# Landing margins per kind of transfer, eight early weight conversions instead of eleven, and the gathers of the row sums issued by GpSimd

## The chip, the core and the metric

The kernel runs on one core of a Trainium2 chip. The metric is the device time of one execution in microseconds (us), the median of several runs. The core has TensorE (PE, matmuls), VectorE (DVE), ScalarE (ACT), GpSimd (POOL) and SyncE (SP, which here only issues DMAs); each works through its own instructions in order and waits at an instruction whose inputs are not there.

## What is computed

Attention on 4 batches of 12 heads (448 tokens, 64 features a head), with scores capped by a tanh, and two feed-forward layers on its output, seen as 1792 tokens of 768 features.

```python
def _attn_ref(q, k, v, cap):
    scores = scale * np.matmul(q, k.transpose(0, 1, 3, 2))
    scores = cap * np.tanh(scores / cap)
    scores = scores - np.max(scores, axis=-1, keepdims=True)
    attn = np.exp(scores)
    attn = attn / (np.sum(attn, axis=-1, keepdims=True) + 1e-09)
    return np.matmul(attn, v).astype(np.float32)

def _moe_ref(x, w_in, w_out):           # d_ff 2048
    h = np.maximum(x @ w_in, 0.0)
    return (h * h @ w_out).astype(np.float32)

def _moe2_ref(x, w_gate, w_val, w_out): # d_ff 1536
    gate = 1.0 / (1.0 + np.exp(-(x @ w_gate)))
    val = x @ w_val
    return (gate * val @ w_out).astype(np.float32)
```

q, k, v are float32; the five weight matrices arrive as float64.

## The kernel before

**Attention** runs over 24 pairs of heads (`pairs`; `last` is 23). For each pair PE makes the scores in four steps (L339, tiles `so`, `si`, `se`), the products with v (L400, `pvo`) and the row sums (L416, `pvs`). ACT makes tanh and exp (`pt`). DVE splits q and k into a rounded part and a rest (L247 and L235, `qkh`, `qkl`) and takes both PSUM results out (L244, `xe`). Then the row sums go round: they sit on single partitions of `xe`, four small DMAs gather them onto 16 partitions (L442, `sg<-xe`, 1.8 KB each), DVE adds and inverts them (L444, L446), the result goes to DRAM (`rd<-rr`), comes back spread over the partitions (L452, `th<-rd`, two DMAs), DVE multiplies (L456), and the product is stored (`xn<-xe`). Two `sg` tiles and two `th` tiles are in use.

**Weights.** Each of the 68 float64 tiles (768 KB) is loaded as pairs of words (L614, `w<-in_w_dram`), turned into float32 by `convert` (L617 on) and stored to DRAM (`s_w<-raw`). Its steps are an absolute value (L627 on DVE during attention; on ACT once the event `mlp` has come, L625), two short DVE steps (L629, L631) and two long ones (L633, L635). Two `w64` and two `raw` tiles exist. `load_w` reads the float32 tiles back when a `pair` tile is free (L661); ACT and DVE split them into `wh` and `wl` (L771, L776) for three matmuls a product (L785, L787, L788, `pb`). `convert_all` (L603) says when a float64 tile is loaded: the first eleven after the pairs 2, 4, ... 22, the rest by the unit of matmuls at which the tile is needed, less 70 units.

**The feed-forward layers** run on four column blocks (stages) with seven products in place of eight; their matmuls are the PE's units.

**The order** of every engine is written before the program runs: a planner (`Flow`) plays the kernel through with durations of its own and writes each engine's instructions in the order in which they come there. A load's landing is `landing` (L162): the transfer at a rate, a latency, and `DLAG`, a margin of 0.3 us. What the planner gets wrong is not mended on the chip: the order stays, and engines wait in it.

Of the kernel before, what the change touches and what calls it, by code (L numbers as in the profile page):

```python
# [19 lines left out]
SP = 512  # L20
NP = H // 2
P = 128
# [7 lines left out]
SR = 32  # L30
EARLY = 150
TWO = (0, 1, 2)
DLAG = 0.3
EDGE = {(0, 2): (0, 0), (1, 0): (0, 2), (1, 2): (1, 0), (2, 0): (1, 2)}
BEGIN = 1
WARM = 3

PT, XE, TH, NV, WB = 2, 6, 2, 2, 4
WSTART, PACE, AHEAD, FIRST = 2, 2, 70, 130
R, G, CP, TM, GX, GY = 5, 5, 3, 3, 8, 4  # L40
HK = CC // 2
HALF = (0, HK, 1)
# [18 lines left out]
class Flow:  # L61
# [2 lines left out]


    LAG = 0.05
    LAND = {"in": (270e3, 1.05), "load": (350e3, 1.15), "store": (350e3, 0.85), "th": (234e3, 1.3), "rd": (350e3, 1.4),
        "sg": (350e3, 0.8)}
    OVER = {"ACT": 0.1, "DVE": 0.08, "SP": 0.0}

    def __init__(self, have):
        self.now, self.heap, self.turn = 0.0, [], 0
        self.have, self.taking = dict(have), {}
        self.done, self.until = {}, []
        self.queue = {e: [] for e in ("ACT", "DVE", "SP")}
        self.free = {e: True for e in self.queue}
        self.pipe = 0.0
        self.changed = lambda: None
        self.jobs = 0
# [34 lines left out]
    def serve(self, engine):  # L114
# [10 lines left out]
        self.at(self.now + length + self.LAG, lambda: self.step(job))  # L125
        self.at(self.now + max(0.02, length - self.OVER[engine]), end)

# [34 lines left out]
    def landing(self, size, kind="load"):  # L162
        rate, after = self.LAND[kind]
        self.pipe = max(self.now + 0.5, self.pipe) + size / rate
        return self.pipe + after + DLAG - self.now


@with_exitstack
def attn_mlp_kernel(ctx: ExitStack, tc: tile.TileContext, qk, v, cap, w1, w2, wg, wv, wo, out):
    nc = tc.nc  # L170
# [8 lines left out]
    def open_pool(name, side, **kw):  # L179
        guard = tc.tile_pool(name=name, bufs=1, side=side, **kw)  # L180
        open_pools[name] = guard, guard.__enter__()

    def close_pool(name):
        open_pools.pop(name)[0].__exit__(None, None, None)

    def T(pool, tag, shape, dt=F32, bufs=1):
        pool = wp if pool == "wp" else open_pools[pool][1]
        return pool.tile(shape, dt, tag=tag, name=tag, bufs=bufs, align_bytes=ALIGN)
# [25 lines left out]
    for j in range(2):  # L214
# [3 lines left out]
    flow = Flow({  # L218
        "sb": 3, "pvo": 1, "pvs": 1, "v": NV, "qkh": 2, "qk": 2, "pt0": PT, "pt1": PT, "xe": XE, "th": TH, "sg": 2,
        "w64": 2, "raw": 2, "pair": 2, "sums": 2, "wh": WB, "tm": TM, **{x: HK for x in FORM.values()},  # L220
        "acc": CC, "gx": GX, "gy": GY, "r": R, "g": G, "cp": CP, "pb": 0})
# [6 lines left out]
    def on(engine, length, write, rank=1):  # L228
        return "on", engine, length, write, rank
# [13 lines left out]
    def copy_ps(out, in_, rank=0):  # L243
        return on("DVE", flow.dve(cols(out)), lambda: nc.vector.tensor_copy(out, in_), rank)  # L244
# [5 lines left out]
    def dma(out, in_, size, kind="load", issue=0.42, rank=1):  # L250
        yield on("SP", issue, lambda: nc.sync.dma_start(out=out, in_=in_), rank)
        yield "for", flow.landing(size, kind)
# [5 lines left out]
    rd = [[dr.tile([2, S], F32, name=f"rd_{b}_{p}") for p in range(NP)] for b in range(B)]  # L258
    xn = [dr.tile([P, B * S], F32, name=f"xn_{p}") for p in range(NP)]
    yn = [dr.tile([P, 2 * BW], F32, name=f"yn_{c}") for c in range(CC)]  # L260
    RP, RN = 16, 2 * S // 16
    pairs = [(b, p) for b in range(B) for p in range(NP)]
    last = len(pairs) - 1
# [156 lines left out]
    def result(n, o):  # L420
        flow.put("pt0")
        flow.put("pt1")
        b, p = pairs[n]
        yield "until", ("xe", n)
        xe = st["xe", n]
        yield copy_ps(xe[:, 1], o)
        flow.put("pvs")
        flow.fire(("pv", n))
        if n == last:
            close_pool("att")  # L430
            open_pool("mlp", "right")
            flow.fire("mlp")


        yield "take", "sg"
        sg = T("out", "sg", [RP, 2, RN], bufs=2)
        rr = T("out", "rr", [RP, RN], bufs=2)
        for x in range(2):
            for j in range(2):
                r0 = (2 * x + j) * SR  # L440
                src = xe[r0:r0 + 1, 1].rearrange("o (i s) -> o i s", s=RN)
                yield on("SP", 0.65, lambda: nc.sync.dma_start(out=sg[j * RP // 2:(j + 1) * RP // 2, x], in_=src), 0)  # L442
        yield "for", flow.landing(0, "sg")
        yield on("DVE", 0.26, lambda: nc.vector.scalar_tensor_tensor(  # L444
            out=sg[:, 0], in0=sg[:, 0], scalar=eps[:RP], in1=sg[:, 1], op0=ALU.add, op1=ALU.add), 0)
        yield on("DVE", 0.49, lambda: nc.vector.reciprocal(rr, sg[:, 0]), 0)  # L446
        yield from dma(rd[b][p].rearrange("r (i s) -> (r i) s", s=RN), rr, 0, "rd", rank=0)
        flow.put("sg")
        yield "take", "th"
        bc = T("out", "th", [P, S], bufs=TH)  # L450
        for j in range(2):
            yield on("SP", 0.52, lambda: nc.sync.dma_start(  # L452
                out=bc[j * D:(j + 1) * D], in_=rd[b][p][j].unsqueeze(0).to_broadcast((D, S))), 0)
        yield "for", flow.landing(P * S * 4, "th")
        xu = xe[:, 0]
        yield on("DVE", flow.dve(S), lambda: nc.vector.tensor_tensor(out=xu, in0=xu, in1=bc, op=ALU.mult), 0)  # L456
        flow.put("th")
        yield from dma(xn[p][:, b * S:(b + 1) * S], xu, P * S * 4, "store", rank=0)
        flow.put("xe")
        flow.fire(("stored", "x", b, p))  # L460
        st["normal"] = st.get("normal", 0) + 1
        if st["normal"] == len(pairs):
            close_pool("out")
            open_pool("sum", "left")
            open_pool("mlp2", "right")
            flow.fire("sum")
# [136 lines left out]
    def convert_all():  # L603
        second_half = [key for key in keys if key[0] not in ("w1", "w2")]
        begin, end = first[second_half[0]] - FIRST, first[second_half[-1]] - AHEAD
        for m, key in enumerate(keys):
            n, u = WSTART + PACE * m, first[key] - AHEAD
            if key in second_half:
                u = min(u, begin + (end - begin) * second_half.index(key) // len(second_half))
            yield "until", ("t", n, 3) if n < last else ("unit", max(u, 0))  # L610
            src, n = source(key)
            yield "take", "w64"
            w64 = T("wp", "w64", [P, CC * P, 2], U32, bufs=2)[:, :n]
            yield on("SP", 0.42, lambda: nc.sync.dma_start(out=w64.rearrange("p n x -> p (n x)"), in_=src.bitcast(U32)), 2)  # L614
            flow.spawn(convert(key, w64, flow.landing(P * n * 8, "in")))

    def convert(key, w64, wait):  # L617
        yield "for", wait
        yield "take", "raw"
        lo, hi = w64[:, :, 0], w64[:, :, 1]  # L620
        n = w64.shape[1]
        raw = T("wp", "raw", [P, CC * P], bufs=2)[:, :n]
        mu = raw.bitcast(U32)
        if "mlp" in flow.done:
            yield act(raw, hi.bitcast(F32), AF.Abs)  # L625
        else:
            yield on("DVE", flow.dve1(n), lambda: nc.vector.tensor_scalar(  # L627
                out=mu, in0=hi, scalar1=0x7FFFFFFF, scalar2=None, op0=ALU.bitwise_and), 2)
        yield on("DVE", flow.dve1(n), lambda: nc.vector.tensor_scalar(  # L629
            out=raw, in0=raw, scalar1=LOW, scalar2=HIGH, op0=ALU.max, op1=ALU.min), 2)  # L630
        yield on("DVE", flow.dve1(n), lambda: nc.vector.tensor_scalar(  # L631
            out=mu, in0=mu, scalar1=5, scalar2=2, op0=ALU.logical_shift_left, op1=ALU.logical_shift_right), 2)
        yield on("DVE", flow.dve(n), lambda: nc.vector.scalar_tensor_tensor(  # L633
            out=mu, in0=lo, scalar=29, in1=mu, op0=ALU.logical_shift_right, op1=ALU.bitwise_or), 2)
        yield on("DVE", flow.dve(n), lambda: nc.vector.scalar_tensor_tensor(  # L635
            out=mu, in0=hi, scalar=0xC0000000, in1=mu, op0=ALU.bitwise_and, op1=ALU.bitwise_or), 2)
        flow.put("w64")
        kind, i = key
        name = f"s_{kind}_{i}".translate({ord(x): "_" if x == "," else None for x in " ,()"})
        scratch[key] = dr.tile([P, n], F32, name=name)  # L640
        yield from dma(scratch[key], raw, P * n * 4, "store")
        flow.put("raw")
        flow.fire(("kept", key))
# [370 lines left out]
    units, groups, first, spot = [], [], {}, {}  # L1014
# [279 lines left out]
```

## Time and profile before

| | |
|---|---|
| median of 3 runs | 1116.3 us (1112.49 to 1118.37) |
| the profiled execution | 1117.42 us, its span 1115.6 us |
| PE busy | 1097.2 us (98% of the span) |
| PE weight loads | 919.6 us (82%) |
| DVE | 899.1 us (81%) |
| ACT | 688.3 us (62%) |
| POOL | 1.1 us, 10 instructions, all memsets of the first 2 us |
| DMA | 227.42 MB, mean 204 GB/s |

A matmul's busy time overlaps the next one's, so a busy share near 100% doesn't tell how much PE lost; its waits and the steps of its sequence do. Attention takes the first 200 us or so, the layers the rest.

### The profile page before, as it was taken

The page shows a single profiled execution, that of the slowest core. Times are in us where ns is not written, and L with a number is a line of the kernel's source. Part 1 is how long each engine was busy: PE and PEld are TensorE (multiplying, and loading weights), DVE is VectorE, ACT ScalarE, POOL GpSimd, SP SyncE. Part 2 cuts the span into 40 slices and gives each one's busy share as a digit, 9 for nine tenths or more (in the row PEclk, how much of TensorE's full clock was granted, in tenths as well). Part 3 has the DMA queues.
Part 4 walks back from the last instruction along what each step waited for, and adds up shares of the span by engine and source line. Part 5 has one row for each costly group of instructions (what it writes and reads, how often), then busy time and mean ns, then how long its engine had stood idle before and what let it go on. Part 6 is the DMA issues. An engine that isn't in the chain of part 4 may idle for free.

```text
span 1115.6 us, 16096 instructions
## 1 busy us (share of the span) xinstructions
PE 1097.2 (98%) x5706; PEld 919.6 (82%) x5706; DVE 899.1 (81%) x1532; ACT 688.3 (62%) x1154; POOL 1.1 (0%) x10
## 2 busy tenths in 40 slices
PE   9999899999999999999999999999999999999998
PEld 4444444798989998999989998998999999999997
DVE  4677999888977488788897999989988767568687
ACT  7889899567464556675656656656545355555352
POOL 0000000000000000000000000000000000000000
PEclk9999999999999999999999999999999999999999
DMA  4678886888875266778896617385438932331322
GB/s 144 210 230 276 253 268 208 266 300 272 260 238 199 65 234 209 286 278 275 319 344 223 223 57 255 135 297 170 163 148 294 323 100 71 104 123 64 100 71 99
DMA packets 83984, 227.42 MB, mean 204 GB/s; under 512 B 11840, under 2 KB 29888, under 8 KB 83904
## 3 DMA queue, kind: packets, MB, share of 16 engines
q1 hardware_dynamic: 83904, 226.40, 60.1%
q8 instruction: 45, 0.74, 0.3%
q14 instruction: 35, 0.29, 0.1%
HBM read 160.24 MB, written 65.95 MB: 203 GB/s over the span
## 4 chain that ended last, share of the span: by engine, by line
PE 75%; DVE 11%; DMA 9%; ACT 3%; issue 2%; SPq 1%; DVEq 0%; POOL 0%; ACTq 0%; POOLq 0%
PE pb L785 21%; PE pb L787 21%; PE pb L788 21%; PE pvo L400 5%; DMA s_w<-raw 2%; PE pvs L416 2%; DVE wl L235 2%; PE se L339 2%; PE so L339 2%; PE si L339 2%; DVE raw L635 1%; ACT wh L232 1%; DVE acc L976 1%; DMA sg<-xe 1%; DVE raw L633 1%
## 5 line engine op out<-in xcount | busy, mean ns | idle before, releaser
L787 PE MATMUL pb<-gx,wh 128*128 128x448 f32 x564 | 205.9, 365 | 1.3 <-DVE gx L235 1.3
L788 PE MATMUL pb<-gx,wh 128*128 128x448 f32 x564 | 205.8, 365 | 0.0
L785 PE MATMUL pb<-gx,wl 128*128 128x448 f32 x564 | 205.1, 364 | 0.0
L785 PE MATMUL pb<-t,wl 128*128 128x448 f32 x480 | 176.2, 367 | 4.3 <-ACT cp L232 4.0
L787 PE MATMUL pb<-t,wh 128*128 128x448 f32 x480 | 175.6, 366 | 0.0
L788 PE MATMUL pb<-t,wh 128*128 128x448 f32 x480 | 175.2, 365 | 0.0
L232 ACT ACTIVATE wh<-pair 128x384 fp32r<-128x384 f32 (+1 forms) x182 | 111.5, 628 | 81.6 <-PE pb L788 63.6
L232 ACT ACTIVATE wh<-sums 128x384 fp32r<-128x384 f32 (+1 forms) x172 | 90.7, 542 | 109.8 <-PE pb L788 88.5
L235 DVE TENSOR_TENSOR wl<-pair,wh 128x384 fp32r<-128x384 f32 (+1 forms) x182 | 123.5, 689 | 26.4 <-ACT wh L232 25.8
L785 PE MATMUL pb<-b,wl 128*128 128x448 f32 x360 | 132.6, 368 | 3.0 <-ACT pb L232 2.8
L787 PE MATMUL pb<-b,wh 128*128 128x448 f32 x360 | 132.5, 368 | 0.0
L788 PE MATMUL pb<-b,wh 128*128 128x448 f32 x360 | 132.0, 367 | 0.0
L235 DVE TENSOR_TENSOR wl<-sums,wh 128x384 fp32r<-128x384 f32 (+1 forms) x172 | 97.7, 579 | 31.9 <-ACT wh L232 31.5
L787 PEld LDWEIGHTS pb<-gx,wh 128*128 128x128 f32 x564 | 105.5, 187 | 10.3 <-DVE gx L235 1.5
L785 PEld LDWEIGHTS pb<-gx,wl 128*128 128x128 f32 x564 | 106.2, 188 | 8.9 <-ACT pb L232 0.6
L788 PEld LDWEIGHTS pb<-gx,wh 128*128 128x128 f32 x564 | 105.9, 188 | 7.9
L785 PEld LDWEIGHTS pb<-t,wl 128*128 128x128 f32 x480 | 90.2, 188 | 15.0 <-ACT cp L232 7.6
L788 PEld LDWEIGHTS pb<-t,wh 128*128 128x128 f32 x480 | 90.2, 188 | 7.5
L787 PEld LDWEIGHTS pb<-t,wh 128*128 128x128 f32 x480 | 90.0, 188 | 7.5
L235 DVE TENSOR_TENSOR gx<-g,gx 128x448 fp32r<-128x448 f32 x124 | 76.0, 619 | 14.7 <-ACT gx L232 13.9
L232 ACT ACTIVATE gx<-g 128x448 fp32r<-128x448 f32 x124 | 70.2, 573 | 20.1 <-DVE g L835 10.0
L232 ACT ACTIVATE raw<-w 128x768 f32<-128x768 f32 x57 | 51.4, 902 | 48.0 <-DMA s_w<-raw 25.3
(105 smaller groups left out, 1799.9 us busy)
## 6 DMA issues: line engine op xcount, KB each, us to landing
w<-in_w_dram SPq DMA_DIRECT2D x32, 768.0 KB
pair<-s_w SPq DMA_DIRECT2D x56, 384.0 KB
s_w<-raw SPq DMA_DIRECT2D x32, 384.0 KB
qk<-in_qk_dram SPq DMA_DIRECT2D x23, 480.0 KB
w<-in_wg_dram SPq DMA_DIRECT2D x12, 768.0 KB
w<-in_wv_dram SPq DMA_DIRECT2D x12, 768.0 KB
w<-in_wo_dram SPq DMA_DIRECT2D x12, 768.0 KB
pair<-s_wo SPq DMA_DIRECT2D x24, 384.0 KB
```

The costliest lines, as they stand in the source:

```text
L232: return on("ACT", flow.act(cols(out)) + extra, lambda: nc.scalar.activation(out=out, in_=in_, func=func, **kw), rank)
L235: return on("DVE", flow.dve(cols(out)), lambda: nc.vector.tensor_tensor(out=out, in0=a, in1=b, op=ALU.subtract), rank)
L339: nc.tensor.matmul(out=sc[:, x, :S], lhsT=w[r, c0:c0 + P], rhs=a[r, :S], start=i == 0, stop=i == 2)
L400: nc.tensor.matmul(out=o[j * D:(j + 1) * D], lhsT=st["v", n][:, c, j], rhs=pt, start=step == 0, stop=step == 3)
L416: nc.tensor.matmul(out=o[r:r + SR], lhsT=head[:, j] if step == 3 else ones, rhs=pt, start=step < 2, stop=step >= 2)
L633: yield on("DVE", flow.dve(n), lambda: nc.vector.scalar_tensor_tensor(out=mu, in0=lo, scalar=29, in1=mu, op0=ALU.logical_shift_right, op1= ...
L635: yield on("DVE", flow.dve(n), lambda: nc.vector.scalar_tensor_tensor(out=mu, in0=hi, scalar=0xC0000000, in1=mu, op0=ALU.bitwise_and, op1= ...
L785: nc.tensor.matmul(out=o, lhsT=wl, rhs=hi, start=first, stop=not stop, skip_group_check=not stop)
L787: nc.tensor.matmul(out=o, lhsT=wh, rhs=lo, start=False, stop=not stop, skip_group_check=not stop)
L788: nc.tensor.matmul(out=o, lhsT=wh, rhs=hi, start=False, stop=not stop or done_, skip_group_check=not stop)
L976: yield on("DVE", flow.dve(w), lambda: nc.vector.tensor_tensor(out=acc, in0=o, in1=acc, op=ALU.add), 0)
```

## The change

It has three parts. Margins: `DLAG` becomes `LATE`, a table for the kind of transfer, with one set before the event `mlp` (float64 tiles 2.5 us, loads 2.0 us) and one after it (float64 tiles 2.0 us); all other kinds keep 0.3 us. Early conversions: the float64 tiles are loaded after the pairs 1, 2, 4, 5, 7, 8, 10 and 11, and the ninth to eleventh follow the rule by units. Gathers: the four `sg<-xe` DMAs of a pair are issued by GpSimd, counted as 1.1 us each by the planner, instead of by SyncE at 0.65 us. The instructions themselves are the same, but for three absolute values that pass from DVE (L627) to ACT.

```diff
-DLAG = 0.3
+LATE = {"w64": 2.5, "load": 2.0}, {"w64": 2.0}
-WSTART, PACE, AHEAD, FIRST = 2, 2, 70, 130
+WHEN, AHEAD, FIRST = (1, 2, 4, 5, 7, 8, 10, 11), 70, 130
-        return self.pipe + after + DLAG - self.now
+        return self.pipe + after + LATE["mlp" in self.done].get(kind, 0.3) - self.now
-                yield on("SP", 0.65, lambda: nc.sync.dma_start(out=sg[j * RP // 2:(j + 1) * RP // 2, x], in_=src), 0)
+                yield on("POOL", 1.1, lambda: nc.gpsimd.dma_start(out=sg[j * RP // 2:(j + 1) * RP // 2, x], in_=src), 0)
-            n, u = WSTART + PACE * m, first[key] - AHEAD
+            n, u = WHEN[m] if m < len(WHEN) else last, first[key] - AHEAD
-            flow.spawn(convert(key, w64, flow.landing(P * n * 8, "in")))
+            flow.spawn(convert(key, w64, flow.landing(P * n * 8, "w64")))
```

The order of PE stays but for one group of four matmuls at the end of attention. SP late in attention, before: `b` and `t` are halves of the first layer's input, `v` the values of a later pair.

```order
L276 DMA qk<-in_qk_dram 128x960
L614 DMA w_1571<-in_w_dram 128x1536
L542 DMA b_1580<-xn_126 128x448
L542 DMA b_1586<-xn_126 128x448
L442 DMA sg<-xe 8x1x56
L452 DMA th<-rd_1_110 64x448
L323 DMA v<-in_v_dram 128x512
```

SP at the same place now:

```order
L276 DMA qk<-in_qk_dram 128x960
L251 DMA rd_1_110<-rr 16x56
L542 DMA t_1567<-xn_123 128x448
L542 DMA b_1584<-xn_126 128x448
L542 DMA b_1591<-xn_126 128x448
L323 DMA v<-in_v_dram 128x512
```

Between the loads of q/k and of v the load of a float64 tile, a gather and a `th` load are gone, and a store and a third load of input stand there. DVE in the same pair, before; `tm`, `t` and `b` are steps on the first layer's input.

```order
L247 CAST qkh<-qk 128x960
L235 TENSOR_TENSOR t_1508<-tm,t_1508 128x448
L235 TENSOR_TENSOR qkl<-qk,qkh 128x960
L235 TENSOR_TENSOR tm<-t_1460,b_1386 128x448
L627 TENSOR_SCALAR raw<-w_1376 128x768
L235 TENSOR_TENSOR tm<-b_1469,tm 128x448
L629 TENSOR_SCALAR raw<-raw 128x768
L631 TENSOR_SCALAR raw<-raw 128x768
L244 COPY xe<-pvo 128x448
```

DVE there now:

```order
L247 CAST qkh<-qk 128x960
L444 SCALAR_TENSOR_TENSOR sg<-sg,eps 16x56
L235 TENSOR_TENSOR qkl<-qk,qkh 128x960
L446 RECIPROCAL rr<-sg 16x56
L235 TENSOR_TENSOR t_1462<-tm,t_1462 128x448
L235 TENSOR_TENSOR t_1501<-tm,t_1501 128x448
L235 TENSOR_TENSOR tm<-b_1421,t_1216 128x448
L235 TENSOR_TENSOR tm<-t_1466,b_1452 128x448
L244 COPY xe<-pvo 128x448
```

The three conversion steps are gone; the eighth conversion has ended two pairs earlier, and no other comes before attention ends. ACT in the first stage of the layers, before, around the absolute value of the 21st float64 tile; `cp` and `pb` are copies of products that PE's next units wait for.

```order
L232 ACTIVATE gx<-g 128x448
L232 ACTIVATE wh<-sums 128x384 x2
L232 ACTIVATE raw<-w_2809 128x768
L232 ACTIVATE cp<-pb_2755 128x448
L232 ACTIVATE wh<-pair 128x768
```

ACT around the same tile now:

```order
L232 ACTIVATE g<-r 128x448
L232 ACTIVATE gx<-g 128x448
L232 ACTIVATE raw<-w_2986 128x768
L232 ACTIVATE wh<-pair 128x768
L232 ACTIVATE r<-r 128x448
```

The absolute value stood right ahead of a `cp`; now a weight split and a step on the layer's inner values follow it.

## Rows read from the trace of the kernel before

**Rows 1.** PE's waits of the whole span: what waited, for whom, total us, times, longest

```profile
PE pb L785 <- ACT cp L232: 4.0, 5, 1.0
PE se L339 <- ACT pt L232: 3.0, 1, 3.0
PE pb L785 <- ACT pb L232: 2.8, 2, 2.1
...
PE pb L787 <- DVE gx L235: 1.3, 1, 1.3
PE pvo L400 <- DMA v<-in_v_dram: 1.0, 1, 1.0
```

**Rows 2.** Busy us (instructions) of PE, PEld, DVE, ACT, POOL, then PE clock, DMA share, GB/s

```profile
104.00:158.00 54.00, 50.01 (x340) 23.58 (x338) 47.08 (x84) 48.22 (x56) 0.00 (x0) 0.97 0.79 252
158.00:190.00 32.00, 32.00 (x222) 14.94 (x220) 30.72 (x57) 30.47 (x36) 0.00 (x0) 1.00 0.73 238
...
120.00:128.00 8.00, 4.98 (x22) 2.01 (x22) 7.97 (x15) 7.37 (x8) 0.00 (x0) 0.79 0.80 255
...
324.00:332.00 8.00, 5.87 (x22) 4.96 (x21) 6.52 (x10) 6.79 (x14) 0.00 (x0) 0.79 0.81 261
```

**Rows 3.** The chain that ended last, attention: start us, us, what; starts of three pairs

```profile
26.61 0.80 PE se L339 x3
...
110.54 0.81 PE si L339 x3
...
162.25 0.80 PE si L339 x3
```

**Rows 4.** ACT's instructions at the first stall: start us, us, what, idle before

```profile
120.64 0.52 ACT L232 ACTIVATE wh<-sums 128x384 fp32r<-128x384 f32 x1 [4.21 <-DVE sums L235]
121.06 1.77 ACT L232 ACTIVATE pt<-pt,capa 128x1792 f32<-128x1792 f32 x1
```

**Rows 5.** DVE's instructions ahead of that stall

```profile
110.43 0.62 DVE L456 TENSOR_TENSOR xe<-xe,th 128x448 f32<-128x448 f32 x1 [1.09 <-DMA th<-rd]
111.99 0.27 DVE L444 SCALAR_TENSOR_TENSOR sg<-sg,eps 16x56 f32<-16x56 f32 x1 [0.93 <-DMA sg<-xe]
...
119.51 0.63 DVE L456 TENSOR_TENSOR xe<-xe,th 128x448 f32<-128x448 f32 x1 [1.46 <-DMA th<-rd]
```

**Rows 6.** SP's issues ahead of the second stall

```profile
147.20 0.43 SPq L614 DMA_DIRECT2D w<-in_w_dram  x1
...
149.33 1.57 SPq L452 DMA_DIRECT2D th<-rd  x1
151.00 0.67 SPq L323 DMA_DIRECT2D v<-in_v_dram  x1
```

**Rows 7.** ACT at a stall of the layers

```profile
265.92 0.92 ACT L232 ACTIVATE raw<-w 128x768 f32<-128x768 f32 x1 [2.06 <-DMA s_w<-raw]
```

**Rows 8.** PE at that stall and at the longest one of the layers

```profile
267.33 0.47 PE L785 MATMUL pb<-t,wl 128*128 128x448 f32 x1 [0.77 <-ACT cp L232]
...
326.95 0.47 PE L785 MATMUL pb<-b,wl 128*128 128x448 f32 x1 [2.13 <-ACT pb L232]
```

**Rows 9.** One line's instructions, the gathers: count, ns min/median/max, first and last start

```profile
L442 SPq DMA_DIRECT2D sg<-xe x96: 619/655/834, 19.8 to 213.6; - x96
```

**Rows 10.** Conversion steps grouped by line, first 200 us: busy us, mean ns, idle before

```profile
L633 DVE SCALAR_TENSOR_TENSOR raw<-w,raw 128x768 uint32<-128x768 uint32 x11 | 10.4, 946 | 0.1
...
L627 DVE TENSOR_SCALAR raw<-w 128x768 uint32<-128x768 uint32 x11 | 6.1, 551 | 8.9 <-DMA w<-in_w_dram 8.9
```

**Rows 11.** The tile `raw` up to 400 us: the absolute values on ACT

```profile
L232 ACT ACTIVATE raw<-w x21: 887/907/928, 203.8 to 343.9; 128x768 f32<-128x768 f32 x21
```

**Rows 12.** SP's longest wait in total, the reloads of weights

```profile
SPq L661 <- DVE wl L235: 279.1, 73, 16.7
```

More of the change, by code (lines that the diff above doesn't have):

```diff
@@ L66 @@
     LAG = 0.05
-    LAND = {"in": (270e3, 1.05), "load": (350e3, 1.15), "store": (350e3, 0.85), "th": (234e3, 1.3), "rd": (350e3, 1.4),
+    LAND = {"in": (270e3, 1.05), "w64": (270e3, 1.05), "load": (350e3, 1.15), "store": (350e3, 0.85), "th": (234e3, 1.3), "rd": (350e3, 1.4),
         "sg": (350e3, 0.8)}
-    OVER = {"ACT": 0.1, "DVE": 0.08, "SP": 0.0}
+    OVER = {"ACT": 0.1, "DVE": 0.08, "SP": 0.0, "POOL": 0.0}
     def __init__(self, have):
@@ L74, in __init__ @@
         self.done, self.until = {}, []
-        self.queue = {e: [] for e in ("ACT", "DVE", "SP")}
+        self.queue = {e: [] for e in ("ACT", "DVE", "SP", "POOL")}
         self.free = {e: True for e in self.queue}
```

## The prediction

> **What bounds the kernel now.** I read PE's waits first, since PE is the engine that never rests long. They come to 12.1 us in the rows shown [rows 1]: 4.0 in attention (3.0 and 1.0) and 8.1 in the layers. Then I read the granted clock by stretch: in two stretches of 8 us it is 0.79 [rows 2], right after PE's two longest waits (3.0 and 2.1 us); PE was at the lower level, 1.2 GHz, for a while, and that cost 0.21 x 8 = 1.7 us each time. So PE lost 12.1 + 3.4 = 15.5 us of 1115.6 to waiting, 1.4%. The change leaves PE's work alone, so this is nearly all it can win, and a profit over 0.5% (5.6 us, about what a measurement of this kernel tells from no change) must take a third of it.
>
> Attention has a beat. The chain's starts of pairs are (110.54 - 26.61) / 11 = 7.63 us apart, with no loss over eleven pairs; the next six take 51.71 us where 6 x 7.63 = 45.8 are due [rows 3]. Attention loses 5.9 us, all between 110 and 162 us (3.0 + 1.0 of waits and 1.7 of clock give 5.7).
>
> The first stall comes from DVE. ACT sat 4.21 us before a weight split (`wh<-sums`) that stands ahead of the exp PE waits for [rows 4], and DVE was late for it because it had waited three times, 3.5 us together, for `th` and `sg` data [rows 5]. DVE has little to spare there: busy 47.1 of 54 us from 104, then 30.7 of 32 [rows 2]. The second stall is a v load that SP issued late, behind a float64 tile, gathers and a slow `th` issue of 1.57 us [rows 6].
>
> In the layers the pattern is another: ACT stands at the absolute value of a float64 tile that has not landed, and a `cp` or `pb` copy that PE needs is queued behind it. At 265.92 ACT had waited 2.06 us [rows 7], and PE lost 0.77 [rows 8]. Five of PE's waits have such a late tile upstream (0.77, 0.40, 2.13, 0.78, 0.67; the largest after a DVE that had fallen behind): 4.75 us, plus the 1.7 of clock after the 2.13, 6.4 in all. The other waits of the layers (two of 1.0 on reloaded weights, 1.3 on a `th`) have nothing to do with float64 tiles.
>
> **Part one, the margins.** They cost no instruction; they move the steps behind a load later in the order of ACT and DVE. After attention the planner counts 2.0 us instead of 0.3 for a float64 tile, 1.7 more. The wait at 265.92 was 2.06, so a little of it would remain were nothing else moved; but the order shows that the `cp` no longer stands behind that tile. I take 70% of the 6.4 us as won: 4.5. The bounds are 6.4, all of it, and a loss of about 3: a new order sets new steps in front of PE's copies, and the waits that the margins don't touch show what one such place costs, 1.0 to 1.3 us; three more of them would be 3.
>
> **Part two, eight conversions early.** A conversion costs DVE three short steps of 0.55 and two long ones of 0.95 during attention (I take the short ones as equal, and the long ones) [rows 10]: 3.55 us. Three fewer are 10.7 us of DVE taken out of attention. They leave the right place: before, conversions go on to the end, beside the steps on the first layer's input, where DVE is 96% busy; in the new order the last one ends in the pair before that work begins. What gets fuller is the middle: between the pairs 5 and 13 I count, from the order's rows and these durations, 58 us of DVE work in 9 x 7.63 = 69, with two pairs in a row a little over 7.63. Before, the six pairs ahead of the first stall were as full. So I don't take all of the 5.9 us: DVE's waits for late float64 tiles (8.9 us [rows 10]) fall under the new margin of 2.5, but the reserve is no larger. I take 4.0, bounds 5.9 and 0.
>
> The three conversions come back in the layers: there each costs ACT 0.9 [rows 11] and DVE 3.0 (without the first step), 11.7 us of work. From 204 to 344 us the tiles follow each other every (343.9 - 203.8) / 20 = 7.0 us [rows 11], so three more run on for some 21 us. Who could wait is the reload of weights; but SP's reloads wait for a free tile, 279 us in 73 waits [rows 12], so they have had a store in hand. I take 0.5 us for a fuller DVE, bounds 0 and 2.7 (ACT's share fully exposed).
>
> **Part three, gathers on GpSimd.** SP loses 96 issues of 0.655 us [rows 9], 63 us out of 194, and its v, q/k and `th` issues no longer queue behind gathers that wait for their sums. Its worth is in the second stall, already counted. The price is unknown: no row shows a DMA issued by GpSimd. The nearest are SP's own issues, 0.655 as the median [rows 9] and 1.57 as the slowest seen [rows 6]. I take 1.1, the middle, which is also what the planner counts; then four issues are 4.4 us of a pair's 7.63, and the sums come where the order expects them. What waits if they come later is DVE at L444, and behind it in order the copies out of PSUM and the q/k splits, and so PE.
>
> **Sum** against the profiled execution: 1117.4 - 4.0 - 4.5 + 0.5 = 1109.4. It lies 1.1 over the median of the runs, so 1108.3 us for the median; 1108. With the bounds of the three terms (all of 5.9 + 6.4 won; or 4.0 lost or not won) this case runs from 1103 to 1113.
>
> **Rivals.** *Given back* (1115, from 1112 to 1118). The margins cure the waits on float64 tiles, but a fresh order has as many of the others, at 1.0 to 1.3 us a place, and the fuller middle of attention loses what the end wins: -4.5 + 3 + 0.5 for the layers and nothing for attention, 1115.3. For it: the waits sit in many places of 1 us, with no one cause. Against: the two largest do have one. That the margins do too little to be seen ends here too.
>
> *GpSimd too dear* (1127, slower). If an issue takes p us there, the sums of a pair come 4 x (p - 1.1) later than planned. DVE idles (54 - 47.1) / 7.1 pairs = 1.0 us a pair [rows 2]; once 4 x (p - 1.1) is over that, from p = 1.35 on, every pair is longer. At p = 1.5 it is 0.6 us a pair, 24 x 0.6 = 14.4 us, and with the layers' 4.0 won, 1116.3 + 14.4 - 4.0 = 1127. From p = 7.63 / 4 = 1.9 GpSimd itself would set the beat. For it: the order expects the gathers close; DVE's conversion steps and q/k casts could hold GpSimd's issues up. Against: GpSimd does nothing else, and 1.35 is a quarter over the planner's number. The Trainium skill speaks against this part: SBUF — State Buffer, in "SBUF: two separate sides", says that the descriptors of a DMA issued from GpSimd are written by GpSimd, which VectorE's two-port operations lock out meanwhile, and that such a DMA of 0.62 us alone took 3.1 beside a VectorE copy. No run here shows it; were every issue 3.1 us, attention would go at 12.4 us a pair, some 115 us longer (an estimate from that page). The rows bound it closer: the casts and short conversion steps are 0.55 to 0.6 us each, at most four in a pair, so they cover less than a third of the time.
>
> *All of it* (1101). Both stalls and all five late tiles go and no new one comes: 1117.4 - 5.9 - 6.4 - 3 (some of the others) - 1.1 = 1101.
>
> **How the numbers follow.** Forecast 0.52, given back 0.25, GpSimd too dear 0.17, all of it 0.06. Faster by over 0.5% means under 1110.7: 0.44 of the forecast's 0.52, the 0.06, and 0.03 of the given-back case, together 0.53. Within 0.5%: 0.08 and 0.20, 0.28. Slower: 0.17 and 0.02, 0.19. The range of 8 in 10 goes from 1101 to 1121: it leaves out the larger part of the dear GpSimd and the better half of the last case. The forecast's own range is 1103 to 1113.
>
> **What would show it.** *Attention:* pair starts 7.63 us apart throughout, and no granted clock under 1.0 near 120 us; if the beat is longer over many pairs and DVE's wait at L444 (`sg<-xe`) is the largest, GpSimd is too dear, and its issue row gives p. *Layers:* ACT's idle time ahead of `raw<-w` falls, and PE's waits on `cp` and `pb` fall from 6.8 us to 2 or 3; if they stay near 6.8 with other releasers, the margins were given back. *Conversions:* 60 absolute values on ACT, 8 on DVE, and reloads that still wait for tiles rather than for stores; a reload that waits for a store ahead of a PE wait would show that three early conversions were missed. The forecast is wrong if DVE in the middle of attention loses a beat as it did at 120 us, or if the first stage of the layers shows new waits over 2 us, each with 1.7 of clock.

## The result, and the profile after

The changed kernel takes **1101.96 us** (median of 4 runs, 1100.5 to 1102.15) where the kernel before takes 1116.18 (4 runs too): a ratio of 0.9873, with a 95% interval from 0.9845 to 0.9901. It is faster by 14.2 us. The forecast was 1108, so its sign was right, its range of 8 in 10 (1101 to 1121) held the time near its low end, and its size was 6 us short: the time lies just under what the prediction calls the forecast's own range, 1103 to 1113. The profiled execution took 1101.87 us, with a span of 1100.1 us.

The page of the changed kernel, busy time and instructions:

```profile
span 1100.1 us, 16188 instructions
...
PE 1090.4 (99%) x5706; PEld 916.3 (83%) x5706; DVE 898.0 (82%) x1529; ACT 689.0 (63%) x1157; POOL 53.6 (5%) x106
```

DVE and ACT do what they did before; POOL has gained its 96 issues. PE's waits, the view that answers [rows 1] (what waited, for whom, total us, times, longest):

```profile
PE pb L785 <- ACT cp L232: 1.5, 3, 0.9
PE pvo L212 <- POOL head L215: 1.3, 1, 1.3
PE si L339 <- DVE qkl L235: 0.9, 2, 0.5
PE pb L785 <- ACT pt L232: 0.7, 1, 0.7
```

The 3.0 for `pt`, the 2.8 for `pb`, the 1.3 for `gx` and the 1.0 for `v` are gone, and `cp` has fallen from 4.0 to 1.5; the 1.3 for `head` is in the first microseconds of both kernels. The stretches of [rows 2] (busy us and instructions of PE, PEld, DVE, ACT, POOL, then PE's clock, DMA share, GB/s):

```profile
104.00:158.00 54.00, 54.00 (x377) 25.14 (x375) 45.79 (x83) 50.67 (x57) 15.06 (x29) 1.00 0.75 235
158.00:190.00 32.00, 31.27 (x209) 14.51 (x207) 22.89 (x44) 29.61 (x33) 10.45 (x20) 1.00 0.55 178
...
324.00:332.00 8.00, 7.72 (x39) 6.79 (x38) 7.03 (x12) 5.45 (x10) 0.00 (x0) 1.00 0.84 258
```

PE is busy for all of the 54 us in which it lost 4.0 before, and the granted clock is 1.00, the level of 2.4 GHz, in both places where it had been 0.79. DVE has 45.79 us of work there where it had 47.08. The chain that ended last, attention (start us, us, what):

```profile
20.44 3.16 PE pvo L400 x16
...
112.00 3.16 PE pvo L400 x16
119.63 3.16 PE pvo L400 x16
...
180.67 3.16 PE pvo L400 x16
```

The beat, 7.63 us a pair as in [rows 3], now holds to the end: (180.67 - 20.44) / 21 = 7.63.

Laying the two traces side by side at the same matmul of PE tells where the 15.5 us between the spans (1115.6 and 1100.1) came from. Attention's first stall with its clock gave 4.9 and the late v load 1.0, and 0.8 was lost at attention's end: 5.1. The places of the five late float64 tiles gave 6.8 with their clock, net of a new wait of 0.5. The `th` wait at 221 us and a reload gave 2.3. The remaining 1.4 arose in the first microseconds, where both kernels issue the same instructions and only the moment at which the granted clock rose differs (10.8 us from the start before, 4.9 now); I don't put that down to the change. The parts add to 15.6 with rounding.

### The profile page after: what moved, and what is told of

Read it like the earlier page. It is cut to its first block, busy times and chain, and to the rows that moved or that the text cites. A ratio compares the mean times of both kernels' runs of the same rounds, so it can differ in the third digit from the quotient of the medians.

```text
span 1100.1 us, 16188 instructions
## 1 busy us (share of the span) xinstructions
PE 1090.4 (99%) x5706; PEld 916.3 (83%) x5706; DVE 898.0 (82%) x1529; ACT 689.0 (63%) x1157; POOL 53.6 (5%) x106
## 4 chain that ended last, share of the span: by engine, by line
PE 87%; DVE 6%; DMA 4%; ACT 2%; issue 1%; SPq 0%; DVEq 0%; ACTq 0%
PE pb L785 24%; PE pb L787 23%; PE pb L788 23%; PE pvo L400 7%; PE pvs L416 3%; DMA s_w<-raw 2%; PE se L339 2%; PE si L339 2%; PE so L339 2%; DVE wl L235 1%; DMA pair<-s_w 1%; DVE raw L633 1%; ACT raw L232 1%; DMA th<-rd 1%; ACT wh L232 1%
## 5 line engine op out<-in xcount | busy, mean ns | idle before, releaser
L235 DVE TENSOR_TENSOR wl<-sums,wh 128x384 fp32r<-128x384 f32 (+1 forms) x172 | 98.4, 581 | 31.0 <-ACT wh L232 30.7
L400 PE MATMUL pvo<-pt,v 128*64 128x448 f32 x384 | 77.9, 546 | 0.2 <-ACT pt L232 0.2
```

Source lines behind the costliest of these rows:

```text
L400: nc.tensor.matmul(out=o[j * D:(j + 1) * D], lhsT=st["v", n][:, c, j], rhs=pt, start=step == 0, stop=step == 3)
```

## The experiments

The ratio is to the kernel before on the same chip (its medians in the three sets of runs were 1117.44, 1117.29 and 1115.42). The ratios and the quotients of these medians differ by up to 0.001; where the text gives an effect both ways, neither figure is the surer. "Side by side" means that two traces are compared at the same matmul of PE.

| kernel | us | ratio (95%) |
|---|---|---|
| `margins_only` | 1113.15 | 0.9952 (0.9936 to 0.9968) |
| `eight_only` | 1118.75 | 1.0011 (0.9992 to 1.0031) |
| `gpsimd_only` | 1108.54 | 0.9911 (0.9885 to 0.9937) |
| `margin_04` | 1124.25 | 1.0060 (1.0035 to 1.0085) |
| `no_gpsimd` | 1104.22 | 0.9875 (0.9854 to 0.9896) |
| `no_eight` | 1107.57 | 0.9907 (0.9884 to 0.9929) |
| `no_margins` | 1108.40 | 0.9911 (0.9890 to 0.9933) |
| `extra_issues` | 1122.79 | 1.0050 (1.0030 to 1.0069) |
| `layers_margin` | 1103.65 | 0.9888 (0.9845 to 0.9931) |
| `after_04` | 1108.90 | 0.9938 (0.9921 to 0.9955) |
| `after_pool055` | 1100.50 | 0.9866 (0.9830 to 0.9901) |
| `after_load2` | 1103.22 | 0.9889 (0.9854 to 0.9924) |

### Each part alone, and a dummy change of the order

**`margins_only`**: the margins alone.

```diff
-DLAG = 0.3
+LATE = {"w64": 2.5, "load": 2.0}, {"w64": 2.0}
```

> The margins alone; eleven early conversions and gathers on SyncE stay. Theory one (the margins cure the late float64 tiles in the layers, 6.4 us in the trace of the kernel before, and some of attention's 5.9): 1107 us, 7 to 12 under the kernel before, PE's waits behind cp and pb copies from 6.8 to under 3 us. Theory two (any newly planned order shakes off the same waits, by luck): no nearer to 1102 than the kernel with a uniform margin of 0.4.

Measured: 4.3 us faster, less than the 7 to 12 expected. Its window in attention and PE's waits show two opposite effects:

```profile
104.00:158.00 54.00, 47.89 (x336) 22.82 (x332) 41.50 (x75) 48.77 (x57) 0.00 (x0) 1.00 0.78 244
```

```profile
PE pvo L400 <- DVE xe L244: 6.6, 5, 2.6
...
PE pb L785 <- ACT cp L232: 1.3, 1, 1.3
PE pb L785 <- ACT pb L232: 0.2, 1, 0.2
```

In the layers the waits on `cp` and `pb` fall from 6.8 us [rows 1] to 1.5, as expected. In attention PE loses 6.1 of 54 us instead of 4.0, and waits for the copy `xe` out of PSUM, which missed the expectation: with the eleven conversions and the gathers where they were, the new order is worse there.

**`eight_only`**: the eight conversions alone.

```diff
-WSTART, PACE, AHEAD, FIRST = 2, 2, 70, 130
+WHEN, AHEAD, FIRST = (1, 2, 4, 5, 7, 8, 10, 11), 70, 130
-            n, u = WSTART + PACE * m, first[key] - AHEAD
+            n, u = WHEN[m] if m < len(WHEN) else last, first[key] - AHEAD
```

> Eight early conversions alone; margin 0.3 for all, gathers on SyncE. Theory one: attention wins 3 to 5.9 us since DVE is no longer full at its end, the layers keep their 8 us of waits or get 1 to 2 more from the three conversions that come back: 1112 us. Rival (the gathers on SyncE are what stalls attention): attention keeps a stall, 1116.

Measured: no difference (1.0011), as the rival had it (1116) and not theory one (1112). DVE has 42.91 us of work in the 54 from 104, four less than before, and PE still loses 3.6 of them:

```profile
104.00:158.00 54.00, 50.44 (x339) 22.67 (x337) 42.91 (x77) 44.96 (x49) 0.00 (x0) 0.97 0.76 254
```

DVE's own waits in attention show why: work was taken from it, but the data that it waits for come no sooner (what waited, for whom, total us, times, longest):

```profile
DVE sg L444 <- DMA sg<-xe: 18.0, 10, 4.0
DVE xe L456 <- DMA th<-rd: 8.9, 8, 3.1
```

Before, the wait for `sg` was 5.1 us. Both gathers and `th` loads are issued by SP. This is the run against which my term for attention falls: I had credited 4.0 us to these conversions.

**`gpsimd_only`**: the gathers on GpSimd alone.

```diff
-                yield on("SP", 0.65, lambda: nc.sync.dma_start(out=sg[j * RP // 2:(j + 1) * RP // 2, x], in_=src), 0)
+                yield on("POOL", 1.1, lambda: nc.gpsimd.dma_start(out=sg[j * RP // 2:(j + 1) * RP // 2, x], in_=src), 0)
```

> Gathers on GpSimd alone; eleven early conversions, margin 0.3. Theory one: SyncE's late v load goes, 1.0 us, DVE stays full at the end of attention, the layers keep their waits: 1113 to 1116. Rival (SyncE's 63 us of gather issues are behind both stalls of attention): attention keeps its beat of 7.63 us throughout, 1110.

Measured: 8.9 us faster, the largest single effect of the three, and the rival's side of the expectation (1110, the beat throughout). Its window and one wait of the layers:

```profile
104.00:158.00 54.00, 54.00 (x379) 25.46 (x377) 51.86 (x92) 52.16 (x60) 14.64 (x27) 1.00 0.85 281
```

```profile
PE pb L785 <- ACT cp L232: 6.1, 5, 3.2
```

With all eleven conversions DVE works for 51.86 of 54 us, 96%, more than before, and PE loses nothing. So a nearly full DVE does not by itself break attention's beat. That leaves DVE waiting for late data [rows 5], which this run supports and doesn't show alone. Side by side with the kernel before, 6.0 us of the gain arose in attention. In the layers the sum of waits on `cp` and `pb` stays, as it should without margins, but not their places: the stall of 2.13 us [rows 8] is gone with its clock, and one of 3.2 us at 210 us, with a granted clock of 0.79 from 206 to 214 us, is new.

**`margin_04`**: a change of the order with no purpose, one margin of 0.4 us for all transfers in place of 0.3. It asks how much a new order moves the time by itself.

```diff
-DLAG = 0.3
+DLAG = 0.4
```

> The kernel before with its uniform margin at 0.4 instead of 0.3 us: no part of the change, only a newly planned order. Theory one (causes that the parts cure): 1112 to 1119, PE's waits again 10 to 16 us with the clock, in other places. Theory two (luck of the order): as likely near 1105 as near 1120.

Measured: 6.8 us slower (1.006), above what either theory gave. PE loses in attention on `xe` and, in the layers, once 4.3 us on a weight remainder:

```profile
PE pvo L400 <- DVE xe L244: 6.2, 7, 1.6
PE pb L785 <- DVE wl L235: 4.3, 1, 4.3
```

So a tenth of a microsecond in the planner's numbers can cost 0.6%, through a few places. Effects of that size need their rows before they are given a cause.

### One part taken from the whole

**`no_gpsimd`**, the changed kernel with the gathers back on SP.

```diff
-                yield on("POOL", 1.1, lambda: nc.gpsimd.dma_start(out=sg[j * RP // 2:(j + 1) * RP // 2, x], in_=src), 0)
+                yield on("SP", 0.65, lambda: nc.sync.dma_start(out=sg[j * RP // 2:(j + 1) * RP // 2, x], in_=src), 0)
```

> The changed kernel with its gathers given back to SyncE; margins and eight early conversions stay. New theory (SyncE's issue time is what attention lacks): attention's beat is broken again, 4 to 7 us lost there, 1109 to 1113. Old theory (the end of attention was short of VectorE time, which eight conversions mend): attention stays whole, 1103.

Measured: 1104.22, a ratio of 0.9875. My new theory, that SP's issue time is what attention lacks, expected 1109 to 1113 with a broken beat, and failed here; the old one, VectorE time, had this outcome. By the medians GpSimd is worth 2.3 us beside the other two parts; by the ratios (0.9873 with it) nothing. Side by side, the traces are 2.4 us apart: 1.4 arose in the first microseconds, ahead of the first gather, 2.1 in the layers, and at the end of attention `no_gpsimd` is 1.0 better. So beside the other two parts GpSimd is worth about 1 us at most, and none of it in attention. The window is whole without it:

```profile
104.00:158.00 54.00, 54.00 (x381) 25.46 (x379) 46.66 (x84) 51.90 (x60) 0.00 (x0) 1.00 0.81 255
```

Nor does DVE wait less for what SP issues than in the kernel before. Its row for `th` from 20 to 200 us, here and then before:

```profile
DVE xe L456 <- DMA th<-rd: 13.6, 14, 2.2
```

```profile
DVE xe L456 <- DMA th<-rd: 7.7, 6, 2.5
```

So the sum of such waits doesn't decide; where they fall in the order does. There are thus two cures for attention, but they don't stand equally firm. In all eight orders of this case with the gathers on GpSimd and no other issues added to SP, PE is busy for 54.00 of the 54 us from 104 and the beat holds. Of the five with the gathers on SP, four break it (47.89 to 50.44 us), and `no_gpsimd` alone, with margins and eight conversions together, keeps it: one order, which no dummy change has tried. Neither margins nor conversions do it alone.

**`no_eight`**, the changed kernel with eleven early conversions.

```diff
-            n, u = WHEN[m] if m < len(WHEN) else last, first[key] - AHEAD
+            n, u = WSTART + PACE * m, first[key] - AHEAD
```

> The changed kernel with eleven early conversions, as before; margins and gathers on GpSimd stay. New theory (the number of early conversions is worth little once SyncE has time): 1101 to 1104. Old theory: attention loses 3 to 6 us again at its end, where VectorE is full, 1105 to 1108.

Measured: 1107.57. The time is in the old theory's range, but what it names does not happen: attention's window is whole with DVE at 50.66 of 54. The loss is at the start of the layers, in PE's waits and in the clock of 216 to 224 us:

```profile
PE pb L787 <- DVE gx L235: 2.6, 2, 1.8
PE pb L785 <- ACT cp L232: 2.1, 2, 1.8
```

```profile
216.00:224.00 8.00, 5.36 (x15) 4.41 (x15) 6.64 (x11) 4.76 (x9) 0.00 (x0) 0.66 0.82 287
```

Side by side with the changed kernel, 7.5 us arise there, through waits of 0.9, 1.8 and 1.8 us and the clock. So eleven conversions cost 5.6 us by the medians, 3.8 by the ratios (whose intervals overlap), at the seam between attention and layers and not at the stall of 120 us. This is one order, and no more than a change with no purpose can move the time; that the number of conversions causes it is not shown.

**`no_margins`**, the changed kernel with 0.3 us for all.

```diff
-LATE = {"w64": 2.5, "load": 2.0}, {"w64": 2.0}
+DLAG = 0.3
```

> The changed kernel with a margin of 0.3 for all kinds; eight early conversions and gathers on GpSimd stay. Theory (the margins cure late float64 tiles in the layers alone): attention whole, PE's waits behind cp and pb copies back at 5 to 9 us, 1107 to 1111. Rival (without them the fuller middle of attention loses its beat too): over 1112.

Measured: 1108.40. Attention is whole; PE's waits in the layers are there again, with late float64 tiles upstream at 260, 318, 671 and 754 us:

```profile
PE pb L785 <- ACT cp L232: 2.6, 4, 1.1
PE pb L785 <- ACT pb L232: 2.5, 3, 1.2
```

That is 5.1 us where the whole has 1.5, and 6.4 us in the time (4.2 by the ratios). Side by side, 4.4 us arose in the layers and 1.4 in the first microseconds, in attention nothing. Over all kernels of this case the margins leave a plain mark: PE's waits on `cp` and `pb` are 0 to 3.6 us in the eight orders that have 2.0 us for float64 tiles in the layers, and 5.1 to 8.1 in the six that don't. Luck of the order is no likely reason for so clean a parting.

### Is it SP's issuing, or the wait for the sums in SP's order?

**`extra_issues`** takes `gpsimd_only` and gives SP 96 small DMAs back which nothing waits for and which wait for no sums: four a pair, 1.8 KB each, from `v` into spare DRAM.

```diff
+        flow.spawn(extra(n))
+    def extra(n):
+        b, p = pairs[n]
+        for x in range(4):
+            spare = dr.tile([8, 56], F32, name=f"spare_{n}_{x}")
+            src = v[b, p].rearrange("p c j d -> p (c j d)")[8 * x:8 * x + 8, :56]
+            yield on("SP", 0.65, lambda: nc.sync.dma_start(out=spare, in_=src), 0)
```

> The kernel with gathers on GpSimd alone, plus 96 small DMAs on SyncE, four a pair in the place of the gathers, which wait for no sums and which nothing waits for (1.8 KB from v to spare tiles in DRAM). Theory one (SyncE's issue time of 63 us is what breaks attention): the beat breaks again, 1114 to 1120. Theory two (it is SyncE standing in its order at a gather whose sums are not there): attention stays whole, 1108 to 1110.

Measured: 1122.79, 14 us over `gpsimd_only` and somewhat over the 1114 to 1120 of theory one, and attention is broken again:

```profile
104.00:158.00 54.00, 50.48 (x350) 23.75 (x346) 45.60 (x82) 48.24 (x55) 13.30 (x24) 1.00 0.80 254
...
158.00:190.00 32.00, 28.19 (x189) 12.84 (x188) 27.77 (x51) 26.61 (x33) 8.85 (x15) 0.95 0.60 192
```

Side by side with `gpsimd_only`, 11 us were lost by the end of attention. The same number of issues as the gathers had, without their waits, is enough to break it in this order. How much room SP has shows in its own waits from 20 to 190 us. Summed over all rows they are 43.3 us before and 43.8 with the extra issues, but 98.9 in `gpsimd_only` and 92.5 in the changed kernel. In `no_gpsimd`, whose attention is whole, they are 44.8: a lack of room puts the beat at risk, and does not always break it. The largest row of SP's waits there, `gpsimd_only` first, then the kernel before:

```profile
SPq L276 <- DVE qkl L235: 30.7, 14, 3.9
```

```profile
SPq L251 <- DVE rr L446: 4.5, 3, 1.7
```

With the gathers gone SP stands 30.7 us at the q/k loads, ahead of a buffer that is not free yet: it is early. Before, its waits are many and short, and behind each stands all that is queued there. What stays open: an issue takes SP's time, it also puts a DMA in flight, and 96 more issues make a newly planned order; this run has all three. It was not tried to add the time alone.

### Which margin, and how much is luck

**`layers_margin`**, the changed kernel with no margins in attention.

```diff
-LATE = {"w64": 2.5, "load": 2.0}, {"w64": 2.0}
+LATE = {}, {"w64": 2.0}
```

> The changed kernel without its margins before the event mlp (2.5 and 2.0 us become 0.3); the margin of 2.0 for float64 tiles in the layers stays. Theory (the margins earn their 6 us in the layers, and with gathers on GpSimd attention needs none): 1101 to 1104, attention whole. Rival (the margins in attention earn it, by setting up the first stage of the layers): 1106 to 1109.

Measured: 1103.65 (0.9888), as the theory had it, attention whole, 2.9 us of `cp` and `pb` waits. Most of what margins earn here is in the layers; the 1.7 us to the changed kernel are inside the intervals.

**`after_04`**, the changed kernel with 0.4 us for all the other kinds of transfer: the dummy change again, from the better order.

```diff
-        return self.pipe + after + LATE["mlp" in self.done].get(kind, 0.3) - self.now
+        return self.pipe + after + LATE["mlp" in self.done].get(kind, 0.4) - self.now
```

> The changed kernel with 0.4 instead of 0.3 us for the kinds that have no margin of their own: a newly planned order and nothing else. If the three parts leave a reserve, its time stays within 4 us of 1102, whereas the same step moved the kernel before by 7. If the changed kernel is a lucky order, 1106 to 1112.

Measured: 1108.90, 7 us worse than the changed kernel, in the range that was put down to a lucky order (1106 to 1112). PE's largest wait and the clock behind it:

```profile
PE pb L785 <- DVE wl L235: 4.2, 1, 4.2
```

```profile
632.00:640.00 8.00, 3.76 (x13) 3.09 (x12) 8.00 (x16) 2.23 (x4) 0.00 (x0) 0.76 0.00 1
```

DVE works without a pause here (8.00 of 8), on the sums of products (`acc`, `t`, `b`) that stand ahead of a weight remainder in its order, and PE waits 4.2 us for that remainder. No step of DVE waits for a landing from 617 to 640 us. The loss is about as large as in `margin_04`, whose wait of 4.3 us stands behind the same kind of sums. The changed kernel owes some of its time to not having such a place.

**`after_pool055`**, the changed kernel with the issue of GpSimd counted at the 0.55 us that its trace shows.

```diff
-                yield on("POOL", 1.1, lambda: nc.gpsimd.dma_start(out=sg[j * RP // 2:(j + 1) * RP // 2, x], in_=src), 0)
+                yield on("POOL", 0.55, lambda: nc.gpsimd.dma_start(out=sg[j * RP // 2:(j + 1) * RP // 2, x], in_=src), 0)
```

> The changed kernel with the planner's price of a gather on GpSimd set to 0.55 us, near the 0.52 that the trace shows, instead of 1.1. If the order only has to be safe, the lower price brings the sums' steps earlier in the order than they land and costs 0 to 4 us: 1102 to 1106. If the price should be right, 1100 to 1102.

Measured: 1100.50 (1099.87 to 1101.64), the lowest of all medians; its ratio, 0.9866, isn't told apart from 0.9873. It is as good as the changed kernel, with a planner that is nearer the chip.

**`after_load2`**, a margin of 2.0 us on the reloads of weights in the layers as well.

```diff
-LATE = {"w64": 2.5, "load": 2.0}, {"w64": 2.0}
+LATE = {"w64": 2.5, "load": 2.0}, {"w64": 2.0, "load": 2.0}
```

> The changed kernel with a margin of 2.0 us for reloads of weights in the layers too. PE's longest wait left in the layers, 0.9 us behind a reload near 546 us, should go: 1100 to 1101. If the later place of those steps starves PE in other places, 1103 to 1108.

Measured: 1103.22, no gain. The reload wait is gone, but PE waits for weight remainders in three new places, at 606, 635 and 670 us:

```profile
PE pb L785 <- DVE wl L235: 2.1, 3, 1.2
```

This is the forecast's rival "given back", in small, and the second half of what was expected (1103 to 1108): 2.1 us of new waits for those removed.

## Why the prediction was right, and where it was short

**What bounds the kernel: right.** PE's waits and the clock behind them were put at 15.5 us and taken as nearly all that could be won. All but 1.4 of the 15.6 found were won there or right beside. One range was not worked out rightly: the bounds of the terms add up to 1104 (1117.4 - 5.9 - 6.4 - 1.1) and 1122 (1117.4 + 3 + 2.7 - 1.1), and not to the 1103 to 1113 that is called the forecast's own.

**The failed step: the cause at the first stall.** The prediction read that DVE had waited 3.5 us for `th` and `sg` [rows 5], and then went by DVE's busy share ("DVE has little to spare there") and credited the conversions with 4.0. `gpsimd_only` has DVE fuller than before and no stall; `eight_only` has it emptier and keeps the stall. The three waits were the reading to follow up: both `sg` and `th` are issued by SP. What the runs show in its place is where the gathers are issued: off SP the beat holds in all eight orders, on SP it breaks in four of five, and 96 idle issues put back on SP (`extra_issues`) break it again. That it is SP's issue time, and not the DMAs in flight or the order, is argued and not shown. The prediction had the price at hand, 96 issues of 0.655, "63 us out of 194" [rows 9], and put its worth at the second stall's 1.0 us alone. The run that does this alone wins 8.9 us, 6.0 of them in attention. That the sum came out near is luck in this term: the part that was credited does nothing alone, another part of the same change bears on the same 5.9 us, and another set of edits (`no_gpsimd`) cures it too. The effects of the three parts therefore don't add, neither alone (-4.3, +1.3, -8.9) nor left out (+6.4 for the margins, +5.6 for the conversions, +2.3 for GpSimd by the medians; by the ratios 4.2, 3.8 and 0.2).

**Attention's size:** 5.1 against 4.0. Part of DVE's fullness had been held against it, which the runs don't bear out.

**Margins: right mechanism, and about the size.** Side by side with the kernel before, the places of the late tiles gave 6.8 against 4.5; side by side with `no_margins`, the margins are worth 4.4 in the layers. The two differ mostly by the largest of the five stalls: 2.13 us with 1.7 of clock before, it is 1.2 without the clock's share in `no_margins` and gone in `gpsimd_only`, neither of which has margins, so part of it went with the new order. `margins_only`, `no_margins` and the waits on `cp` and `pb` over all orders show the mechanism from both sides. The sign that I gave held: ACT's idle time ahead of `raw<-w` fell. Its group of instructions, before and after (busy us, mean ns, then the idle time before them and what ended most of it):

```profile
L232 ACT ACTIVATE raw<-w 128x768 f32<-128x768 f32 x57 | 51.4, 902 | 48.0 <-DMA s_w<-raw 25.3 <-DMA s_wo<-raw 10.3 <-DMA w<-in_wo_dram 3.7
```

```profile
L232 ACT ACTIVATE raw<-w 128x768 f32<-128x768 f32 x60 | 54.0, 900 | 34.0 <-DMA s_w<-raw 25.9 <-DVE raw L635 3.6 <-DMA s_wv<-raw 2.2
```

It is 21.4 us in `margins_only` and 53.1 in `no_margins`. But it isn't a sure sign: `no_gpsimd`, with all margins, has 51.0 and yet only 3.6 us of PE's waits on `cp` and `pb`. What stands behind the tile counts too, as in the order shown ahead of the prediction, where a weight split replaced a `cp`.

**Three conversions coming back: +0.5 assumed, nothing found.** The change keeps 60 absolute values on ACT and 8 on DVE as forecast, and SP's reloads still wait mostly for tiles (255.9 us against 279.1 [rows 12]):

```profile
SPq L661 <- DVE wl L235: 255.9, 75, 15.7
```

In the one order with eleven beside the other two parts, it is eleven that is slower, by 3.8 to 5.6 us (`no_eight`).

**The others: 0 assumed, 2.3 found.** The `th` wait and a reload, which I had called untouched, went as well. That `th` load is one of SP's issues; which part removed it the runs don't tell, and none need have: in `margin_04`, a change with no purpose, PE's wait on `gx` is gone as well.

**GpSimd too dear: no.** The gathers of the changed kernel on GpSimd, the answer to [rows 9] (count, ns min/median/max, first and last start; then the landing of these DMAs):

```profile
L442 POOL DMA_DIRECT2D sg<-xe x96: 518/518/1076, 18.7 to 199.0; - x96
...
DMA to landing us min/median/max: 1.5/3.0/6.5
```

The issue takes 0.52 us, the mean is 52.5 / 96 = 0.55: below my lower bound of 0.655, and half of the 1.1 that I took. From p = 1.35 on it would have hurt; only single issues come near, and DVE has no wait for `sg` left. The Trainium skill (SBUF — State Buffer, "SBUF: two separate sides") gives 3.1 us for such a DMA beside a VectorE copy. As a price of the issue this is not borne out here: the slowest of 96 beside a busy VectorE took 1.08. The 3.0 us from issue to landing are near it, but what part VectorE has in them no run tells. Another page of the Trainium skill, DMA: Bandwidth & Descriptors, in "Issuing engines are not separate DMA queues", says that issuing from several engines saves only sequencer time, which is usually small relative to the DMA itself. Here 96 issues of 0.655 us are 63 us of SP's time [rows 9], a third of attention.

**Given back (1115) and all of it (1101).** The time came out where *all of it* had it, at a chance of 0.06. The chance was too low since I took a fresh order to have as many bad places as the old one. `margin_04` and `after_04` show that the fear had a size, 6.8 and 7 us, yet both have a place that the changed kernel happens not to have.

## What to carry to other kernels

Count the queue that issues DMAs like an engine: its issues times their duration, against the stretch, and if an engine "has little to spare" look first at what it waits for and who issues that. A margin in a planner pays where the planner was wrong, and its effect shows more surely in the waits of what is queued behind the late step than in the step's own wait. Where an order is written ahead, time a change with no purpose (a margin moved by 0.1 us) beside the real one: here it moved the time by 0.6%, more than the margins earn alone, and one part alone or left out says little until its rows are read. Where many orders have been run, compare all with a part to all without it, as for the margins and the gathers here; that tells a cause from a lucky order.

## What the runs showed of the hardware

A small gather issued by GpSimd took 0.52 us of its sequencer as the median of the changed kernel, less than the same gather on SP (0.655 as the median in the kernel before), though VectorE was busy beside it for 85% of the 54 us from 104, and for 96% in `gpsimd_only`, where the median is 0.521; it landed 1.5 to 6.5 us after its issue.

A single wait of PE of 4.2 us, in `after_04`, ended in a stretch of 8 us with a granted clock of 0.76, and the stretch of 216 to 224 us in `no_eight`, with waits of 0.9 and 1.8 us, had 0.66: PE at the lower level, 1.2 GHz, for part of them. The length of one wait doesn't decide alone: one of 1.7 us in `eight_only` ended in a stretch with 0.79 (140 to 148 us), and around one of 2.25 us in `extra_issues` the clock was 1.00 (136 to 146). No wait under 1 us shows such a loss in the changed kernel, whose mean clock over the span is 1.0.
